# Weight pair sums moved from GpSimd to VectorE, and the step tables of a fused attention and feed-forward kernel set anew

## The chip, the cores and the metric

The kernel runs on one core of a Trainium2 chip. The metric is the device time of one execution in microseconds (us). A core has five engines that run side by side, each with its own queue of instructions in a fixed order: TensorE (PE; PEld is its weight load), VectorE (DVE), ScalarE (ACT), GpSimd (POOL) and SyncE (SP), which issues all transfers (DMA) here. An engine whose next instruction has to wait holds up all that stand behind it in its queue.

## The reference

```python
def _attn_ref(q, k, v):                       # (8, 12, 448, 64) each, float32
    scores = scale * np.matmul(q, k.transpose(0, 1, 3, 2)) - np.log(S)
    attn = 1.0 / (1.0 + np.exp(-scores))
    return np.matmul(attn, v)

def _moe_ref(x, w_ch1, w_ch2):                # x (8, 448, 768), w 768x3072 and 3072x768
    X = np.fft.fft(np.fft.fft(x, axis=1), axis=2)
    u = x + np.real(X)
    un = (u - mean(u)) / np.sqrt(var(u) + 1e-06)
    return u + np.maximum(un @ w_ch1, 0.0) @ w_ch2
```

The weights arrive as float64 and are read as pairs of 32-bit words. Sigmoid attention over 96 heads, a real part of a two-dimensional Fourier transform, a row norm and a two-layer feed-forward net follow each other.

## The kernel before

**First part, to about 365 us.** A loop over even ticks `t` (one tick is one 128-row block of scores) issues per round: last round's stores (`sp_next`), last round's ACT reads (`act_next`), a list of small steps that the table `extra` holds for this tick (sorted by rank), the scores, the values, and some matmuls of the Fourier stage. Into the same ticks go the loads of the weights' words (`weight_load`, tile `wr`, L400), a running maximum of each (`weight_max`, L408), and for 30 weight blocks the conversion from float64 to float32 in three steps (`convert`: ACT L416, DVE L418, DVE L421) into a tile `t` of three buffers, from where it is stored to `t_dram` (L433). A new conversion can start on ACT only when the store of the third last one has landed. `STORES` says for the stores of `u` and of `t` whether they join `sp_next` (issued at the start of the next round) or `sp_later` (one round after that). The norm of the first 512 rows (`NORMS`, `token_norm` with c = 0) ends in four pairs of DMA transposes (L591), issued from SP as well. The Fourier stage's results go from PSUM through ACT (`A`, L331; `Q`, L342) and DVE (`u`, L368).

**Second part, 365 to 400 us.** The rest of the Fourier stage runs beside the first up projections; a list `prepq` feeds one weight step per round.

**Third part, from 400 us.** The work is cut into blocks `P`, each of 14 ticks: seven ticks issue an up projection (`fast_up`, nine matmuls of 256 columns, `psf`, L1073), the others a down projection (`down_plain`, `po`, L946, for the first 512 rows; `fast_down`, `pso`, L1145, after that). `UPS`, `PIECES` and `DOWN_TICKS` say which tick issues what. Products go through two PSUM banks (`a` and `b`): ACT copies (`X`, L1088; `F`, L1095) and DVE sums (`F`, L1084) must read a bank before TensorE may write to it again, a few ticks later; so a late ACT or DVE stops TensorE.

The up and down products use sums and differences of weight quarters. These pair sums (`pair_sum`, L634, four for each pair of weight blocks, 128x384 float32, both inputs in SBUF) run on GpSimd: 10 pairs by `w1_pair` (tile `t`), 2 by `w1_rest` (tile `tp`), 12 by `w2_sums` (tile `cb`); 96 in all. After them comes a scaled float16 copy on ACT (`high`, L623) and its remainder on DVE (`low`, L626, tile `ws`). `to_float32` turns the words of further blocks on the way (`w1_turn`, L416, L418, L421 with tile `r`). GpSimd also does the small norm operations (`mv`, L516 to L540) of the later rows.

Where each of these steps stands is set by tables of tick numbers: `at_tick(P, k, fn)` puts a step at tick `k` of block `P` (negative: before it), and within a tick by the fraction. Blocks 2 to 11 handle the first 512 rows (to about 545 us), blocks 12 to 23 the next 512 rows with the second weight's pair sums made on the way, and from block 24 on (about 724 us) all weights are loaded ready-made.

Of the kernel before, what the change touches and what calls it, by code (L numbers as in the profile page):

```python
# [13 lines left out]
ALU = mybir.AluOpType  # L14
# [44 lines left out]
TICKS = 14  # L59
DOWN_TICKS = (1, 3, 5, 7, 9, 10, 13)  # L60
DOWN_FROM = 5
STORES = (1, 1)
MAX_STEP = (0, 0, 0, 0, 0, -4.0, 0, 0, 0, 0, 0, 0, 0, 0, 0, 0, 0, 0, 0, 0, 0, 0, 0, 4.0, 0, 0, 0, 0, 0, 0, 0, 0, 0, 0, 0, 0, 0, 0, 0, 0, 0, 0, 0, 0, 0, 0, 4.0, 0)
CONV_STEP = (0, 2, 4, 0, 2, 4, 0, 2, 4, 0, 2, 4, 0, 2, 4, 0, 0.0, 4, 0, 2, 4, 0, 2, 4, 0, 2, 4, 0, 2, 4, 0, 2, 4, 0, 2, 4, 0, 2, 4, 0, 2, 4, 0, 2, 4, 0, 2, 2.0, 0, 2, 4, 0, 2, 4, 0, 2, 4, 0, 2, 4, 0, 2, 4, 0, 2, 4, 0, 2, 4, 0, 2, 4, 0, 2, 4, 0, 2, 4, 0, 2, 4, 0, 2, 4, 0, 2, 4, 0, 2, 4, 0, 2, 4, 0, 2, 4, 0, 2, 4, 0, 2, 4, 0, 2, 4, 0, 2, 4, 0, 2, 4, 0, 2, 4, 0, 2, 4, 0, 2, 4, 0, 2, 4, 0, 2, 4, 0, 2, 4, 0, 2, 4, 0, 2, 4, 0, 2, 4, 0, 2, 4, 0, 2, 4)
CONV_RANK = (4, 8.0, 14.0)
CAST_STEP = (0, 0, 0, 0, 0, 0, 0, 0, 0, 0, 0, 0, 0, 0, 0, 0, 0, 0, -2.0, 0, 0, 0, 0, 0, 0, 0, 0, 0, 0, 0, 0, 0, 0, 0, 0, 0, 0, 0, 0, 0, 0, 0, 0, 0, 0, 0, 0, 0, 0, 0, 0, 0, 0, 0, 0, 0, 0, 0, 0, 0, 0, 0, 0, 0, 0, 0, 0, 0, 0, 0, 0, 0, 0, 0, 0, 0, 0, 0, 0, 0, 0, 0, 0, 0, 0, 0, 0, 0, 0, 0, 0, 0, 0, 0, 0, 0)
W1P_AT = (1.25, 3, 4, 5.75, 6, 6.25, 9.0, 11.0, 13.0)
TURN_AT = (2, 4, 4.0, 5.75, 8.0, 8.0)
WORDS_AT = (4.0, 2.5)
W2P_AT = (-4.75, 8.0, 8.0, 9.0)  # L70
# [18 lines left out]
def spectral_attention_ffn(tc, q, k, v, w1, w2, cd, cs, ident_in, out):  # L89
    nc = tc.nc  # L90
# [7 lines left out]
    with ExitStack() as top:  # L98
# [19 lines left out]
        if True:  # L118
# [433 lines left out]
            def token_norm(c, tp, n, rows_in, stage, dma, e):  # L552
# [63 lines left out]
            prep = {}  # L616
# [229 lines left out]
        with ExitStack() as fast, ExitStack() as plain, ExitStack() as pairs, ExitStack() as words_in:  # L846
# [24 lines left out]
            def w1_pair(p, n):  # L871
                t = prep[0, p]
# [18 lines left out]
            def w1_rest(p, n):  # L891
# [26 lines left out]
            def w2_sums(P, n):  # L918
# [448 lines left out]
```

## Time and profile before

| | |
|---|---|
| median of 3 runs | 1572.38 us (1570.44 to 1575.49) |
| profiled execution, whole | 1571.36 us |
| its span, first to last instruction | 1569.6 us |
| busy share: PE, PEld, DVE, ACT, POOL | 98%, 68%, 71%, 51%, 23% |
| mean granted TensorE clock | 0.996 |

The span is 1.76 us shorter than the execution it belongs to; what lies around it is taken as the same for both kernels. The profile is read by stretches of time, since the five parts have different limits: a busy share over the whole span mixes them.

### The profile page before, as it was taken

How to read it: one execution, taken by the hardware profiler on the slowest of the kernel's cores; microseconds unless marked ns; L12 is line 12 of the kernel's file. 1: busy time of each engine (PE TensorE's matmuls, PEld its weight loads, DVE VectorE, ACT ScalarE, POOL GpSimd, SP SyncE). 2: the span in 40 equal slices, each digit the busy share in tenths (PEclk: the TensorE clock that was granted, in tenths of full speed). 3: DMA queues.
4: the chain of work that ended last, by engine and by line, in shares of the span. 5: the costliest groups of instructions: out<-in, count | busy, mean ns of one | idle time of the engine just before them, and what ended most of it. 6: DMA issues, size and time to landing. Idle time of an engine off the chain costs nothing.

```text
span 1569.6 us, 27940 instructions
## 1 busy us (share of the span) xinstructions
PE 1534.7 (98%) x11338; PEld 1067.9 (68%) x11338; DVE 1119.4 (71%) x1802; ACT 795.4 (51%) x1125; POOL 367.8 (23%) x446
## 2 busy tenths in 40 slices
PE   9999999899999999999999999999999999999998
PEld 4555555455667676777777777777777777777775
DVE  2668878777788856887767676767666766766567
ACT  6777777673566536543544244533543364324231
POOL 3645656541344625240000000000000000000000
PEclk9999999999999999999999999999999999999999
DMA  7878798955898998997797578667857676856544
GB/s 236 318 272 301 232 363 288 311 205 183 319 288 323 288 353 295 324 259 272 260 275 213 208 305 236 232 222 286 257 224 235 259 258 238 270 228 235 198 173 151
DMA packets 162996, 407.83 MB, mean 260 GB/s; under 512 B 87489, under 2 KB 101554, under 8 KB 144690
## 3 DMA queue, kind: packets, MB, share of 16 engines
q1 hardware_dynamic: 162866, 406.04, 75.8%
q8 instruction: 89, 1.46, 0.4%
q14 instruction: 41, 0.34, 0.1%
HBM read 319.49 MB, written 66.85 MB: 246 GB/s over the span
## 4 chain that ended last, share of the span: by engine, by line
PE 78%; DVE 8%; ACT 4%; POOL 4%; issue 3%; DMA 2%; SPq 1%; DVEq 0%; ACTq 0%; POOLq 0%
PE psf L1073 29%; PE pso L1145 28%; PE av L265 7%; PE sc L206 5%; PE psd L328 2%; POOL cb L634 2%; PE po L946 2%; DVE ws L626 1%; PE sc L240 1%; DVE F L1084 1%; ACT ws L623 1%; PE pss L338 1%; PE psx L361 1%; POOL t L634 1%; PE psh L656 1%
## 5 line engine op out<-in xcount | busy, mean ns | idle before, releaser
L1073 PE MATMUL psf<-ut,ws 128*128 128x256 f16 x5166 | 643.1, 273 | 14.1 <-DVE F L1084 8.4
L1073 PEld LDWEIGHTS <-ws 128*128 128x128 f16 x5166 | 505.6, 98 | 131.4 <-issue 18.6
L1145 PE MATMUL pso<-ws,H 128*128 128x384 f16 x3024 | 559.8, 326 | 1.0 <-DVE H L1084 0.9
L1145 PEld LDWEIGHTS <-H 128*128 128x128 f16 x3024 | 295.9, 98 | 154.1 <-DVE H L1084 1.7
L1159 DVE TENSOR_TENSOR acc<-pso,acc 128x384 f32<-128x384 f32 x399 | 220.4, 554 | 99.6 <-PE pso L1145 94.2
L1088 ACT ACTIVATE X<-psf 128x256 f32<-128x256 f32 x246 | 93.7, 381 | 261.0 <-PE psf L1073 260.1
L1084 DVE TENSOR_TENSOR F<-X,psf 128x256 f32<-128x256 f32 x246 | 102.6, 417 | 145.0 <-PE psf L1073 93.7
L218 ACT ACTIVATE a<-sc 128x900 f32<-128x900 f32 x168 | 148.8, 925 | 57.3 <-PE sc L206 56.9
L1084 DVE TENSOR_TENSOR H<-F,H 128x1024 f16<-128x1024 f32 (+1 forms) x144 | 156.3, 1120 | 17.3 <-ACT H L1113 17.2
L1113 ACT ACTIVATE H<-F 128x1792 f16<-128x1792 f32 x72 | 122.1, 1697 | 69.7 <-DVE F L1084 68.9
L265 PE MATMUL av<-a,vr 128*64 128x450 f32 (+1 forms) x768 | 139.9, 547 | 0.0
L529 POOL TENSOR_SCALAR mv<-mv 128x2 f32<-128x2 f32 x12 | 4.2, 346 | 564.5 <-ACT U L528 564.3
L1084 DVE TENSOR_TENSOR F<-F 128x256 f32<-128x256 f32 x288 | 109.8, 419 | 12.8 <-ACT F L1102 10.4
L199 DVE TENSOR_TENSOR lo<-qk,hi 128x834 fp32r<-128x834 f32 (+2 forms) x50 | 58.9, 1181 | 63.7 <-ACT hi L181 54.6
L265 PEld LDWEIGHTS av<-a,vr 128*64 128x64 f32 (+1 forms) x768 | 44.8, 136 | 82.0 <-issue 77.0
L1102 ACT ACTIVATE F<-F 128x768 f32<-128x768 f32 x72 | 60.7, 843 | 75.1 <-DVE F L1084 75.1
L1095 ACT ACTIVATE F<-psf 128x256 f32<-128x256 f32 x82 | 31.3, 382 | 133.0 <-PE psf L1073 133.0
L946 PE MATMUL po<-w2q,H 128*128 128x512 f16 (+1 forms) x528 | 93.5, 326 | 0.0
L289 POOL TENSOR_TENSOR eo<-xT 128x450 f32<-128x450 f32 x37 | 54.7, 1494 | 98.4 <-ACT xT L277 98.4
L634 POOL TENSOR_TENSOR t<-t 128x384 f32<-128x384 f32 x40 | 53.0, 1324 | 95.3 <-DVE ws L626 65.2
L634 POOL TENSOR_TENSOR cb<-cb 128x384 f32<-128x384 f32 x48 | 56.2, 1196 | 73.9 <-DMA cb<-t_dram 53.3
L946 PEld LDWEIGHTS <-H 128*128 128x128 f16 x528 | 51.7, 98 | 24.5
(122 smaller groups left out, 1627.5 us busy)
## 6 DMA issues: line engine op xcount, KB each, us to landing
ws<-w_dram SPq DMA_DIRECT2D x132, 1344.0 KB, 7.1
wr<-w_in SPq DMA_DIRECT2D x48, 768.0 KB, 7.2
r<-w_in SPq DMA_DIRECT2D x18, 768.0 KB, 9.6
w_dram<-ws SPq DMA_DIRECT2D x10, 1344.0 KB, 9.4
t_dram<-t SPq DMA_DIRECT2D x30, 384.0 KB, 6.6
qk<-q_in SPq DMA_DIRECT2D x48, 225.0 KB, 6.7
qk<-k_in SPq DMA_DIRECT2D x48, 224.0 KB, 5.3
vr<-v_in SPq DMA_DIRECT2D x24, 448.0 KB, 4.2
```

The costliest lines, as they stand in the source:

```text
L206: nc.tensor.matmul(ps[:, j, :SQ], split[g, kn][1][h, c * 128:(c + 1) * 128], split[g, qn][0][h], start=(n == 0), stop=(n == 2))
L218: nc.scalar.activation(a, ps[:, :, :SQ], AF.Sigmoid, bias=-math.log(S), scale=1.0 / math.sqrt(D))
L265: nc.tensor.matmul(av[1][j * D:(j + 1) * D, :SQ], vr[k, v0:v0 + D], a[k, j], start=(av[0] == 0), stop=(av[0] == 3))
L634: e.tensor_tensor(out=t[:, o], in0=t[:, x], in1=t[:, y], op=op)
L946: nc.tensor.matmul(po[n][:, at:at + hi - lo], h[:, x, j, i * 128:(i + 1) * 128], w[:, y, c0 + lo:c0 + hi], start=(p == j == m == at == 0), ...
L1073: nc.tensor.matmul(ps, w[:, i, a, m * 128:(m + 1) * 128], ut[j][:, b + (c == 0), m], start=(no in (1, 2, 5) and m == n == 0), stop=(m == n ...
L1084: nc.vector.tensor_tensor(out=o, in0=x, in1=y, op=op)
L1088: later(0, lambda: nc.scalar.activation(X[:, k], ps, AF.Copy))
L1102: nc.scalar.activation(F[:, 0:3], F[:, 0:3], AF.Relu)
L1113: nc.scalar.activation(h_tile(P)[:, 0], F[:, 1:8], AF.Copy)
L1145: nc.tensor.matmul(ps[:, :384], H[:, x, a, tp * 128:(tp + 1) * 128], w[:, y, b], start=(j == group[0] and n == 0), stop=(j == group[-1] an ...
L1159: later(0, lambda: nc.vector.tensor_tensor(out=to, in0=ps[:, :384], in1=to, op=ALU.add))
```

## The change

`ON_POOL` names, for the eight kinds of pair sum (four of the first weight, four of the second) and four kinds of norm subtraction, the engine. Only the last sum of the second weight's four stays on GpSimd; the other kinds run on VectorE. So 84 of 96 sums move, and 12 stay. (The norm subtractions were on VectorE before and stay there.) `STORES` goes from `(1, 1)` to `(0, 0)`. All tables of ticks for weight, norm and conversion steps get new numbers; `PIECES` moves two down pieces of the first-row blocks from tick 5 to tick 3.

```diff
-NORMS = ((66, 74, 76, 80, 84, 88, 94), (108, 114, 116, 120, 124, 128, 134))
+NORMS = ((66, 74, 76, 80, 86, 88, 94), (108, 114, 116, 116, 124, 124, 136))
...
-STORES = (1, 1)
+STORES = (0, 0)
+ON_POOL = (0, 0, 0, 0, 0, 0, 0, 1, 0, 0, 0, 0)
...
-CONV_RANK = (4, 8.0, 14.0)
+CONV_RANK = (4, 10.0, 16.0)
...
-TURN_AT = (2, 4, 4.0, 5.75, 8.0, 8.0)
+TURN_AT = (2, 3.75, 4.0, 6.75, 9.0, 10.0)
 WORDS_AT = (4.0, 2.5)
-W2P_AT = (-4.75, 8.0, 8.0, 9.0)
-REST_AT = (-12.25, 0, 0.0, 3.0, 3, 5, 7, 9)
+W2P_AT = (-5.75, 6.25, 8.0, 9.75)
+REST_AT = (-12.25, 0, 0.0, 0.0, 3, 5, 6.0, 8.0)
 RESID_AT = (3, 8)
-SUMS_AT = (-4, 2, 3.0, 6, 8, 10, 10, 11.25, 15.25)
-SUMS2_AT = (-17.0, -10.0, -7.75, -5.0, -3.0, 2.0, 6.25, 9.75, 12.75)
-LOAD_AT = (8.25, 2.0, -2.0)
+SUMS_AT = (-5.0, 2, 3.0, 6, 8, 10, 10, 11.25, 14.25)
+SUMS2_AT = (-19.0, -9.25, -7.0, -4.25, -2.25, 2.0, 7.0, 10.5, 13.5)
+LOAD_AT = (8.25, -4.75, -4.0)
 NORM0_AT = (6.0, 62.0)
 NORM_AT = (34.0, 90)
-NORM_STEP = (0, 13.0, 17.0, 19.0, 22.0, 22.25, 23.5, 29.25, 29.5, 31.25, 33.25, 34.5, 36.5, 41.5, 43.5)
-PIECES = {1: 0, 3: 0, 5: 5, 7: 1, 10: 5, 13: 1}
+NORM_STEP = (0, 13.0, 17.0, 22.0, 25.0, 25.25, 28.5, 32.25, 32.5, 34.25, 36.25, 37.5, 39.5, 44.5, 49.5)
+PIECES = {1: 0, 3: 2, 5: 3, 7: 1, 10: 5, 13: 1}
...
+            def eng(n):
+                return (nc.vector, nc.gpsimd)[ON_POOL[n]]
...
-                    pair_sum(0, t, n - 2, nc.gpsimd)
+                    pair_sum(0, t, n - 2, eng(n - 2))
...
-                    pair_sum(0, prep[0, p], n - 1, nc.gpsimd)
+                    pair_sum(0, prep[0, p], n - 1, eng(n - 1))
...
-                    pair_sum(1, prep[1, P], n - 1, nc.gpsimd)
+                    pair_sum(1, prep[1, P], n - 1, eng(n + 3))
```

The left-out lines are tables with a number for each of 48 weight maxima, 144 conversion steps and 96 casts, of which six, two and none change in value. In the changed file, lines after 62 stand one further down, lines after the new function `eng` four.

The first place is SP's queue near the second pair of transposes of the second norm block (some 287 to 298 us in the trace). `t_3044` is a converted weight block; before the change its store stood here:

```order
L400 DMA wr<-w_in 128x1536
L591 DMA_TRANSPOSE ut<-un_3083 128x12x128 x2
L172 DMA vr<-v_in 128x896
L400 DMA wr<-w_in 128x1536
L433 DMA t_dram<-t_3044 128x768
L166 DMA qk<-k_in 128x448
L167 DMA qk<-q_in 128x450
L433 DMA t_dram<-t_3085 128x768
```

In the changed kernel the same block is called `t_3048` and the transposes take `un_3131`:

```order
L401 DMA wr<-w_in 128x1536
L434 DMA t_dram<-t_3048 128x768
L173 DMA vr<-v_in 128x896
L401 DMA wr<-w_in 128x1536
L595 DMA_TRANSPOSE ut<-un_3131 128x12x128 x2
L434 DMA t_dram<-t_3086 128x768
L167 DMA qk<-k_in 128x448
L168 DMA qk<-q_in 128x450
```

The store of this block has moved from behind the two transposes to ahead of them, and ahead of two loads; the next store (`t_3085`, now `t_3086`) stands behind the transposes in both.

The second place is DVE's queue in the blocks of the first 512 rows, from the first half of `low` to the second bank-freeing sum `F<-X,psf` after it (`t_` and a number is a weight pair on its way, `r` the words it is made from, `w2q` the second weight's copy, `U` the norm's rows). Before, in block 4 (some 433 to 447 us):

```order
L626 SCALAR_TENSOR_TENSOR ws<-t_4394,wsc,ws 128x1152
L418 TENSOR_SCALAR t_4570<-t_4570 128x768
L421 SCALAR_TENSOR_TENSOR t_4570<-r,t_4570 128x768
L418 TENSOR_SCALAR t_4570<-t_4570 128x768
L421 SCALAR_TENSOR_TENSOR t_4570<-r,t_4570 128x768
L626 SCALAR_TENSOR_TENSOR w2q<-t_4477,wsc,w2q 128x1536
L574 TENSOR_TENSOR U<-U 128x384 x2
L1084 TENSOR_TENSOR F<-X,psf 128x256
L626 SCALAR_TENSOR_TENSOR ws<-t_4394,wsc,ws 128x1536
L574 TENSOR_TENSOR U<-U 128x384 x2
L1084 TENSOR_TENSOR F<-X,psf 128x256
```

In the changed kernel:

```order
L630 SCALAR_TENSOR_TENSOR ws<-t_4394,wsc,ws 128x1152
L419 TENSOR_SCALAR t_4557<-t_4557 128x768
L638 TENSOR_TENSOR t_4394<-t_4394 128x384
L422 SCALAR_TENSOR_TENSOR t_4557<-r,t_4557 128x768
L638 TENSOR_TENSOR t_4394<-t_4394 128x384 x3
L630 SCALAR_TENSOR_TENSOR w2q<-t_4469,wsc,w2q 128x1536
L419 TENSOR_SCALAR t_4557<-t_4557 128x768
L1088 TENSOR_TENSOR F<-X,psf 128x256
L422 SCALAR_TENSOR_TENSOR t_4557<-r,t_4557 128x768
L630 SCALAR_TENSOR_TENSOR ws<-t_4394,wsc,ws 128x1536
L578 TENSOR_TENSOR U<-U 128x384 x2
L1088 TENSOR_TENSOR F<-X,psf 128x256
```

Four sums (L638) now stand ahead of the first of these two bank-freeing sums, the two halves of the words' turn (L419, L422) are drawn apart, and the norm's first two subtractions have moved behind that bank-freeing sum.

The third place is DVE's queue in block 14, the first even block in which the second weight's sums (`cb`) are made while the earlier ones run out (some 583 to 597 us). Before:

```order
L1084 TENSOR_TENSOR F<-X,psf 128x256
L1084 TENSOR_TENSOR F<-F 128x256 x4
L1084 TENSOR_TENSOR F<-X,psf 128x256
L1084 TENSOR_TENSOR H<-F,H 128x1024
L1084 TENSOR_TENSOR H<-F,H 128x768
L1084 TENSOR_TENSOR F<-X,psf 128x256
L626 SCALAR_TENSOR_TENSOR ws<-cb,wsc,ws 128x1536
L1084 TENSOR_TENSOR F<-X,psf 128x256
```

In the changed kernel:

```order
L1088 TENSOR_TENSOR F<-X,psf 128x256
L1088 TENSOR_TENSOR F<-F 128x256 x4
L638 TENSOR_TENSOR cb<-cb 128x384
L1088 TENSOR_TENSOR F<-X,psf 128x256
L638 TENSOR_TENSOR cb<-cb 128x384
L1088 TENSOR_TENSOR H<-F,H 128x1024
L638 TENSOR_TENSOR cb<-cb 128x384
L1088 TENSOR_TENSOR H<-F,H 128x768
L638 TENSOR_TENSOR cb<-cb 128x384 x2
L1088 TENSOR_TENSOR F<-X,psf 128x256
L638 TENSOR_TENSOR cb<-cb 128x384
L630 SCALAR_TENSOR_TENSOR ws<-cb,wsc,ws 128x1536
```

Six sums of two weight pairs now stand among the bank-freeing sums; the two that close each set of four are still on GpSimd.

## Rows read from the trace of the kernel before

**Rows 1.** Busy time per engine by stretch: us, busy us, granted clock, DMA share, GB/s.

```profile
0.00:365.00 365.00, 351.57 (x2411) 192.26 (x2412) 260.81 (x340) 263.60 (x340) 197.27 (x170) 0.99 0.81 274
365.00:400.00 35.00, 32.29 (x196) 20.94 (x195) 25.81 (x39) 13.92 (x17) 4.00 (x4) 1.00 0.67 226
400.00:540.00 140.00, 132.37 (x988) 96.33 (x986) 118.21 (x113) 88.88 (x112) 71.38 (x72) 1.00 0.93 309
540.00:700.00 160.00, 153.74 (x1161) 113.80 (x1159) 113.10 (x173) 81.08 (x119) 57.90 (x73) 0.99 0.92 306
700.00:1520.00 820.00, 820.00 (x6286) 614.80 (x6284) 564.73 (x1072) 338.57 (x528) 37.26 (x128) 1.00 0.71 245
```

**Rows 2.** TensorE's own waits: engine, line, releaser, us in total, times, longest.

```profile
PE psf L1073 <- DVE F L1084: 8.4, 11, 1.6
PE psf L1073 <- ACT X L1088: 4.5, 7, 2.3
...
PE pss L338 <- ACT A L331: 3.7, 1, 3.7
```

**Rows 3.** Timeline 286 to 306: start, us, engine, line, tiles, idle before and releaser.

```profile
286.60 0.95 DVE L421 SCALAR_TENSOR_TENSOR t<-wr,t 128x768 int32<-128x768 int32 x1
...
287.45 7.23 SPq L591 DMA_TRANSPOSE ut<-un  x2
...
296.52 0.42 SPq L433 DMA_DIRECT2D t_dram<-t  x1
...
302.24 0.89 ACT L416 ACTIVATE t<-wr 128x768 f32<-128x768 f32 x1 [5.79 <-DMA t_dram<-t]
```

**Rows 4.** Busy time per engine, two short stretches with a lower clock.

```profile
304.00:308.00 4.00, 3.62 (x14) 2.27 (x14) 1.73 (x3) 4.00 (x7) 3.92 (x3) 0.50 1.04 410
...
600.00:604.00 4.00, 4.00 (x23) 2.57 (x22) 2.51 (x4) 3.67 (x6) 0.00 (x0) 0.65 1.02 404
```

**Rows 5.** Pair sums on GpSimd and a like VectorE row: busy us, mean ns.

```profile
L634 POOL TENSOR_TENSOR cb<-cb 128x384 f32<-128x384 f32 x48 | 56.2, 1196 | 73.9 <-DMA cb<-t_dram 53.3 <-DVE acc L1159 19.6
...
L634 POOL TENSOR_TENSOR t<-t 128x384 f32<-128x384 f32 x40 | 53.0, 1324 | 95.3 <-DVE ws L626 65.2 <-DMA u_dram<-u 27.9
...
L1199 DVE TENSOR_TENSOR acc<-acc 128x384 f32<-128x384 f32 x70 | 38.5, 550 | 0.2
```

**Rows 6.** Conversion's last step, whole run: shortest, median, longest ns.

```profile
L421 DVE SCALAR_TENSOR_TENSOR t<-r,t x18: 959/1633/1643, 395.9 to 520.6; 128x768 int32<-128x768 int32 x18
```

**Rows 7.** VectorE groups, 400 to 700: busy us, mean ns, idle before.

```profile
L421 DVE SCALAR_TENSOR_TENSOR t<-r,t 128x768 int32<-128x768 int32 x16 | 23.5, 1467 | 0.5
...
L1084 DVE TENSOR_TENSOR H<-F,H 128x768 f16<-128x768 f32 x9 | 11.7, 1305 | 0.0
```

**Rows 8.** The same table, 700 to 1520, with GpSimd nearly idle.

```profile
L1084 DVE TENSOR_TENSOR H<-F,H 128x768 f16<-128x768 f32 x60 | 57.8, 964 | 0.0
```

**Rows 9.** Timeline 437.5 to 446.5, columns as in rows 3.

```profile
438.08 1.95 ACT L543 ACTIVATE U<-U,mv 128x768 f32<-128x768 f32 x2 [2.62 <-POOL mv L540]
...
441.53 2.33 DVE L626 SCALAR_TENSOR_TENSOR w2q<-t,wsc,w2q 128x1536 f16<-128x1536 f32 x1 [3.54 <-ACT w2q L623]
...
445.30 1.14 PE L1073 MATMUL psf<-ut,ws 128*128 128x256 f16 x9 [1.59 <-DVE F L1084]
```

**Rows 10.** Timeline 585 to 600, columns as in rows 3.

```profile
586.08 9.72 POOL L634 TENSOR_TENSOR cb<-cb 128x384 f32<-128x384 f32 x8 [17.89 <-DMA cb<-t_dram]
...
593.80 1.57 ACT L623 ACTIVATE ws<-cb,wsc 128x1536 f16<-128x1536 f32 x1 [4.79 <-POOL cb L634]
...
595.41 2.00 DVE L626 SCALAR_TENSOR_TENSOR ws<-cb,wsc,ws 128x1536 f16<-128x1536 f32 x1 [5.03 <-ACT ws L623]
...
599.32 0.97 PE L1073 MATMUL psf<-ut,ws 128*128 128x256 f16 x4 [2.27 <-ACT X L1088]
```

**Rows 11.** Waits of SyncE's DMA queue, columns as in rows 2.

```profile
SPq L400 <- DVE t L421: 28.9, 8, 7.9
```

**Rows 12.** The page's DMA issues: KB each, median us to landing.

```profile
ws<-w_dram SPq DMA_DIRECT2D x132, 1344.0 KB, 7.1
```

More of the change, by code (lines that the diff above doesn't have):

```diff
@@ L61 @@
 DOWN_FROM = 5
-STORES = (1, 1)
-MAX_STEP = (0, 0, 0, 0, 0, -4.0, 0, 0, 0, 0, 0, 0, 0, 0, 0, 0, 0, 0, 0, 0, 0, 0, 0, 4.0, 0, 0, 0, 0, 0, 0, 0, 0, 0, 0, 0, 0, 0, 0, 0, 0, 0, 0, 0, 0, 0, 0, 4.0, 0)
-CONV_STEP = (0, 2, 4, 0, 2, 4, 0, 2, 4, 0, 2, 4, 0, 2, 4, 0, 0.0, 4, 0, 2, 4, 0, 2, 4, 0, 2, 4, 0, 2, 4, 0, 2, 4, 0, 2, 4, 0, 2, 4, 0, 2, 4, 0, 2, 4, 0, 2, 2.0, 0, 2, 4, 0, 2, 4, 0, 2, 4, 0, 2, 4, 0, 2, 4, 0, 2, 4, 0, 2, 4, 0, 2, 4, 0, 2, 4, 0, 2, 4, 0, 2, 4, 0, 2, 4, 0, 2, 4, 0, 2, 4, 0, 2, 4, 0, 2, 4, 0, 2, 4, 0, 2, 4, 0, 2, 4, 0, 2, 4, 0, 2, 4, 0, 2, 4, 0, 2, 4, 0, 2, 4, 0, 2, 4, 0, 2, 4, 0, 2, 4, 0, 2, 4, 0, 2, 4, 0, 2, 4, 0, 2, 4, 0, 2, 4)
@@ L65 @@
-CONV_RANK = (4, 8.0, 14.0)
-CAST_STEP = (0, 0, 0, 0, 0, 0, 0, 0, 0, 0, 0, 0, 0, 0, 0, 0, 0, 0, -2.0, 0, 0, 0, 0, 0, 0, 0, 0, 0, 0, 0, 0, 0, 0, 0, 0, 0, 0, 0, 0, 0, 0, 0, 0, 0, 0, 0, 0, 0, 0, 0, 0, 0, 0, 0, 0, 0, 0, 0, 0, 0, 0, 0, 0, 0, 0, 0, 0, 0, 0, 0, 0, 0, 0, 0, 0, 0, 0, 0, 0, 0, 0, 0, 0, 0, 0, 0, 0, 0, 0, 0, 0, 0, 0, 0, 0, 0)
+STORES = (0, 0)
+ON_POOL = (0, 0, 0, 0, 0, 0, 0, 1, 0, 0, 0, 0)
+MAX_STEP = (0, 0, 0, 0, 0, -4.0, 0, 0, -2.0, 0, 0, 0, 0, 0, 0, 0, 0, -4.0, 0, 0, 0, 0, 0, 4.0, 2.0, 0, 0, 0, 0, 0, 0, 0, 0, 0, 0, 0, 0, 0, 0, 0, 0, 0, 0, 4.0, -2.0, 0, 4.0, 4.0)
@@ new lines @@
+CONV_STEP = (0, 2, 4, 0, 2, 4, 0, 2, 4, 0, 2, 4, 0, 2, 4, 0, 0.0, 4, 0, 2, 4, 0, 2, 4, 0, 2, 4, 0, 2, 4, 0, 2, 4, 0, 2, 4, 0, 2, 4, 0, 2, 4, 0, 2, 4, 0, 2, 2.0, 0, 2, 4, 0, 2, 4, 0, 2, 4, 0, 2, 4, 0, 2, 4, 0, 2, 4, 0, 2, 4, 0, 2, 4, 0, 2, 4, 0, 2, 4, 0, 2, 4, 0, 2, 4, 0, 2, 4, 0, 2, 4, 0, 2, 4, 0, 2, 4, 0, 2, 4, 0, 2, 4, 0, 2, 4, 0, 2, 4, 0, 2, 2.0, 0, 2, 4, 0, 2, 4, 0, 2, 4, 0, 2, 4, 0, 4.0, 4, 0, 2, 4, 0, 2, 4, 0, 2, 4, 0, 2, 4, 0, 2, 4, 0, 2, 4)
+CONV_RANK = (4, 10.0, 16.0)
+CAST_STEP = (0, 0, 0, 0, 0, 0, 0, 0, 0, 0, 0, 0, 0, 0, 0, 0, 0, 0, -2.0, 0, 0, 0, 0, 0, 0, 0, 0, 0, 0, 0, 0, 0, 0, 0, 0, 0, 0, 0, 0, 0, 0, 0, 0, 0, 0, 0, 0, 0, 0, 0, 0.0, 0, 0, 0, 0, 0, 0, 0, 0, 0, 0, 0, 0, 0, 0, 0, 0, 0, 0, 0, 0, 0, 0, 0, 0, 0, 0, 0, 0, 0, 0, 0, 0, 0, 0, 0, 0, 0, 0, 0, 0, 0, 0, 0, 0, 0)
@@ L572, in token_norm @@
                 elif n < 11:
-                    for o, x, y in (((4, 0, 2), (5, 1, 4)), ((6, 1, 0), (7, 3, 5)))[n - 9]:
-                        nc.vector.tensor_tensor(out=U[:, o], in0=U[:, x], in1=U[:, y], op=ALU.subtract)
+                    for k, (o, x, y) in enumerate((((4, 0, 2), (5, 1, 4)), ((6, 1, 0), (7, 3, 5)))[n - 9]):
+                        (eng(2 * n + k - 10) if c else nc.vector).tensor_tensor(out=U[:, o], in0=U[:, x], in1=U[:, y], op=ALU.subtract)
                 else:
```

## The prediction

> **What bounds the kernel now.** I read first the busy time by stretch [rows 1]. TensorE is the engine that sets the end: from 700 us on it is busy for 820.0 of 820.0 us, so nothing can be won there. Its idle time lies in the earlier stretches: 13.4 us to 365, 2.7 to 400, 7.6 to 540 and 6.3 to 700, together 30 us, beside some at the end that the change does not touch. So the change can win about 2% of the span at most, and it wins only what it takes from these four stretches.
>
> Then I asked what ended TensorE's waits [rows 2]. After 400 us it waits for a PSUM bank that DVE or ACT has not yet read: 8.4 us for DVE's sums `F`, 4.5 us for ACT's copies `X`. In the first part one wait of 3.7 us stands out, for ACT's copy `A`.
>
> Its cause is in the timeline [rows 3]. ACT wanted to start a conversion and found no free buffer: it sat idle for 5.79 us until a store of `t` had landed, and the copy `A` stood behind it in its queue. DVE had finished that block at 287.55 (286.60 plus 0.95), but SP issued its store only at 296.52, since two transposes kept SP's queue for 7.23 us from 287.45 on. After the pause the granted clock was 0.50, so TensorE ran at 1.2 instead of 2.4 GHz for 304 to 308, which loses 2.0 us more; after the pause near 597 us it was 0.65 for 4 us, a loss of 1.4 us [rows 4].
>
> After 400 us DVE is the tight engine: busy 118.2 of 140 us, then 113.1 of 160 [rows 1]. In block 4 the chain is: ACT waits 2.62 us for GpSimd's norm operations, so `w2q` on DVE starts 3.54 us late, the sum `F` stands behind it, and TensorE stops for 1.59 us [rows 9]. In block 14 it is GpSimd's sums: eight of `cb` take 9.72 us from the landing of their load, ACT waits 4.79 us for them, DVE 5.03 us for ACT, and TensorE stops for 2.27 us behind a copy that stood after this [rows 10].
>
> **The change part by part.**
>
> *The sums.* 84 of 96 sums leave GpSimd, where one takes 1.32 us (`t`) or 1.20 us (`cb`) [rows 5]. On DVE the nearest row is an addition of the same shape with both inputs in SBUF, 0.55 us [rows 5]. Four belong to the pair done before 400 us, so 80 come to DVE between 400 and 710 us: 44 us. Two weight chains become shorter by this: four sums took some 4 x 1.2 to 1.3 us, and take 2.2 us of DVE time.
>
> *What DVE gets back.* While GpSimd works, DVE's operations with two SBUF inputs take longer: the conversion's last step takes 959 ns at best and 1633 ns in the median [rows 6]; its mean between 400 and 700 us is 1467 ns for 16, so 8.1 us are lost there [rows 7]. The 768-element remainder of `H` takes 1305 ns there and 964 ns where GpSimd is nearly idle: 9 x 0.34 = 3.1 us [rows 7, 8]. These two groups give 11 us, the lower bound; if each of the 80 sums cost its neighbours what the conversion step shows on average (0.51 us), it is 41 us. I take 20, nearer to the lower end, since many of DVE's operations there read PSUM and GpSimd often ran beside those. DVE's load then rises by 24 us (3 to 33), from 231 to 255 of 300 us.
>
> The Trainium skill, "SBUF — State Buffer", section "Who interferes with whom", says that a DVE instruction with two SBUF inputs and a GpSimd instruction that reads SBUF exclude each other for a whole instruction. By that rule a sum could hold DVE up for all of its time and more would come back than I take; the trace agrees in the sign, and its 0.67 us between best and median [rows 6] is less than a sum's length.
>
> *Blocks 2 to 11, 400 to 540 us (7.6 us idle).* About 42 of the moved sums fall here: 118.2 + 42 x 0.55 - about 14 of the 20 us = 127 of 140 us. That fits, but with little room. What TensorE loses there are not averages but long or late operations ahead of `F`. Without sums on GpSimd its norm operations have nothing of that kind beside or ahead of them, the scaling stands three ticks later, and the norm's subtractions no longer stand ahead of the bank-freeing sum in block 4: the 1.59 us wait [rows 9] and its like go. `PIECES` gives ACT's copy of the first product two pieces' time before its bank is written again. I take 5 of 7.6 us; the bounds are 7.6 won and 8 lost (DVE full, below).
>
> *Blocks 12 to 22, 540 to 700 us (6.3 us idle, 1.4 us of clock).* The sums of each `cb` pair cost DVE 1.65 us and GpSimd about 1 us, in place of 9.72 us for two pairs in a row, so ACT no longer waits 4.79 us [rows 10]. What is late next is the load itself: a sum on DVE waits for `cb` with the bank-freeing sums behind it, where before only GpSimd waited (17.89 us, harmless by itself) [rows 10]. That load landed at 586.08, about when the block's first sum is due, and its issue now stands one or two ticks earlier; I expect waits under 1 us. An even block holds six sums (3.3 us) and an odd one none, and the norm's steps move to the odd ones. DVE: 113.1 + 21 - 6 = 128 of 160 us. I take 4.5 of 7.7 us; bounds 7.7 won, 3 lost.
>
> *The stores.* With `STORES` at 0 a store is issued one round earlier. The block of [rows 3] is stored ahead of the two transposes, so some 6 to 9 us earlier, and the wait of 5.79 us goes. But the next block's store stays behind the transposes, and without the pause its buffer is wanted sooner; I expect a shorter wait of ACT there. Of 3.7 us [rows 2] and 2.0 us of clock I take 4.2; bounds 0 and 5.7. The rest of the idle 13.4 us is DVE being late by about a microsecond at a time; the new places of maxima and norm steps shift that, I take nothing, and 4 us either way as bounds.
>
> *365 to 400 us.* Four sums (2.2 us) come onto DVE, which was busy 25.8 of 35 us [rows 1]; the earlier stores of `u` free its buffers sooner. Together nothing, with 2 us either way.
>
> *The steady stretch.* `LOAD_AT` puts two weight loads next to each other. A load of 1344 KB lands in 7.1 us [rows 12], and two blocks of TensorE work lie between issue and use; DMA is busy for 0.71 there [rows 1]. Hidden; if a load were late it would show as a wait of TensorE for `ws`, and each us counts fully. The later norm steps there lie beside a DVE that is 69% busy.
>
> *Sum:* 4.2 + 5 + 4.5 + 0 = 13.7 us. From the profiled execution's 1571.36 us that leaves 1557.7; the runs' median is 1.0 us above that execution, so 1558.7, and I say 1558.5 us.
>
> **The rivals.**
>
> *DVE becomes the bound (slower).* Place: blocks 2 to 11. If nothing comes back of DVE's lengthened operations, its work is 118.2 + 23.1 = 141 us in a stretch of 140, and part of its idle 21.8 us, in which it waits for ACT in order, cannot be filled. With half of it kept, the stretch takes 152 us: 12 lost instead of 5 won. The rest unchanged but for the stores (4.2) and nothing won in blocks 12 to 22, the time is 1572.4 + 12 - 4.2 = 1580. It decides from the point where DVE's added work there exceeds what it has idle beyond those waits, about 11 us net. For it: 84% busy already. Against it: the lengthened steps of [rows 6, 7].
>
> *The move changes nothing.* What GpSimd waited for, DVE now waits for, and stops go to other places. Blocks 2 to 22 keep their 14 us, only the stores win: 1568. The Trainium skill, "Perfetto Trace Analysis", section "Optimizing Scalar/DVE Operations", warns that moving work between these two engines might not help, as they share a read port. That rule would end here; the rows of the lengthened operations [rows 7, 8] rather speak for the one that pays less being DVE alone.
>
> *The stores give back what they win.* They now stand ahead of loads and hold SP until DVE has finished a block; such waits were 28.9 us in 8 already, the longest 7.9 [rows 11]. If the loads of `qk` behind them come late, the 4.2 us won become some 4 lost: 1567. Against it: those loads were issued long ahead, and none is named among TensorE's waits.
>
> *All of it is won.* If every sum gives DVE back 0.51 us or more, its load falls or stays, and all 7.6, 7.7 and 5.7 us go, perhaps 3 more of the first part: 1572.4 - 24 = 1548.
>
> **How the numbers follow.** My forecast (1552 to 1566) has 0.42. All won: 0.16, faster. The stores give back: 0.12, at the edge of faster. Nothing changes: 0.14, counted as the same. DVE full: 0.16, slower. A measurement of this kernel can tell 0.3% (4.7 us) from no change, so faster is below 1567.7 and slower above 1577.1: 0.70, 0.14 and 0.16. The range from 1547 to 1576 leaves out most of the last case and a little at the lower end.
>
> **What would show it.** Right: no 5.79 us wait of ACT for a store and a granted clock near 1.00 between 300 and 312; the conversion's step near 0.96 us after 400; waits of `psf` for DVE and ACT of a few us together; still 100% of TensorE's time busy in the steady stretch, begun some 13 us earlier. Wrong: DVE busy for over 95% between 400 and 540 with more waits of `psf` behind it; sums of `cb` on DVE waiting for their load; waits for `ws` loads after 700 us; or another store that lands late.

## The result, and the profile after

| | before | after |
|---|---|---|
| median | 1571.79 us (1570.44 to 1575.49, 4 runs) | 1548.56 us (1547.14 to 1549.52, 4 runs) |
| profiled execution, its span | 1571.36, 1569.6 | 1549.52, 1547.7 |
| busy share PE, DVE, POOL | 98%, 71%, 23% | 99%, 73%, 17% |
| mean granted clock | 0.996 | 0.998 |

The ratio is 0.985 (95% interval 0.983 to 0.987): 23.2 us won, where 13.9 were forecast. The time lies 1.6 us above the lower end of the stated range, and below the 1552 to 1566 us that my own sum had for itself.

Busy time by stretch of the changed kernel, columns as in [rows 1]:

```profile
0.00:365.00 365.00, 358.35 (x2477) 199.26 (x2478) 266.61 (x350) 267.56 (x346) 196.26 (x170) 1.00 0.83 280
365.00:400.00 35.00, 33.41 (x200) 20.62 (x199) 28.49 (x42) 14.14 (x17) 0.00 (x0) 1.00 0.79 273
400.00:540.00 140.00, 137.58 (x1033) 101.32 (x1031) 119.97 (x154) 91.86 (x115) 14.13 (x30) 0.99 0.95 319
540.00:700.00 160.00, 157.67 (x1214) 118.45 (x1212) 132.01 (x227) 84.84 (x121) 23.42 (x42) 1.00 0.93 310
700.00:1520.00 820.00, 819.76 (x6288) 614.81 (x6286) 560.02 (x1072) 338.03 (x527) 33.18 (x120) 1.00 0.71 243
```

TensorE's idle time in the four stretches was 13.4, 2.7, 7.6 and 6.3 us; it is 6.7, 1.6, 2.4 and 2.3. The steady stretch is full as before. DVE's load from 400 to 700 us rose from 231 to 252 us. That stretch holds more of the work than before, since all of it starts earlier. Over the whole execution DVE is busy for 1130.6 us instead of 1119.4: the 84 sums bring 46 us, and 11 us remain, so some 35 us were given back.

Fixed bounds shift against the work, so I also cut the run at events of TensorE. The view of one line's instructions gives each line's first and last start (us, behind the shortest, median and longest time in ns); first in the kernel before, then in the changed one:

```profile
L265 PE MATMUL av<-a,vr x768: 535/541/959, 10.8 to 360.7; 128*64 128x450 f32 x144, 64*64 64x450 f32 x48
L1073 PE MATMUL psf<-ut,ws x5166: 269/273/417, 399.1 to 1538.8; 128*128 128x256 f16 x199
L946 PE MATMUL po<-w2q,H x528: 272/326/379, 408.6 to 580.1; 128*128 128x512 f16 x88, 128*128 128x256 f16 x88
L1145 PE MATMUL pso<-ws,H x3024: 322/326/524, 588.4 to 1565.6; 128*128 128x384 f16 x189
```

```profile
L266 PE MATMUL av<-a,vr x768: 535/541/769, 11.1 to 352.4; 128*64 128x450 f32 x144, 64*64 64x450 f32 x48
L1077 PE MATMUL psf<-ut,ws x5166: 269/273/422, 389.0 to 1517.0; 128*128 128x256 f16 x199
L950 PE MATMUL po<-w2q,H x528: 272/326/631, 398.4 to 563.9; 128*128 128x512 f16 x88, 128*128 128x256 f16 x88
L1149 PE MATMUL pso<-ws,H x3024: 322/326/337, 572.7 to 1543.9; 128*128 128x384 f16 x189
```

In the changed kernel the last value product starts at 352.4 us, the first up product at 389.0, the last down product of the first rows at 563.9, and the last one of all at 1543.9. So the four parts were 360.7, 38.4, 181.0 and 985.5 us long and are now 352.4, 36.6, 174.9 and 980.0: won are **8.3 us** in the first part, **1.8** in the second, **6.1** in blocks 2 to 11, **5.5** after them. The third cut lies at the last down product of the first rows, some 24 to 40 us behind the 540 us of the forecast, so the third part takes in some of the stretch of blocks 12 to 22. These parts are used for every run below; each comes from the one execution that was profiled.

TensorE's waits, columns as in [rows 2]:

```profile
PE psf L1077 <- ACT X L1092: 3.1, 3, 2.2
PE psx L362 <- DVE u L369: 2.9, 3, 2.0
PE psf L1077 <- DVE F L1088: 1.9, 3, 1.2
PE psi L709 <- DVE u L706: 1.7, 1, 1.7
...
PE sc L207 <- DVE lo L200: 0.8, 1, 0.8
```

The wait of `pss` for the copy `A` is gone, and the waits for `F` went from 8.4 to 1.9 us. The timeline answers to [rows 3]:

```profile
284.12 0.38 SPq L434 DMA_DIRECT2D t_dram<-t  x1
...
287.07 9.96 SPq L595 DMA_TRANSPOSE ut<-un  x2
...
294.18 0.91 ACT L417 ACTIVATE t<-wr 128x768 f32<-128x768 f32 x1
...
297.13 0.53 SPq L434 DMA_DIRECT2D t_dram<-t  x1
```

The store now leaves before the two transposes, although these hold SP for 9.96 us. The next one leaves at 297.13 behind them, as I had feared, but the next waits of ACT for a landed store are short, 0.48 and 1.08 us. The granted clock was 1.00 from 292 to 312, against 0.50 at 304 to 308 [rows 4].

DVE's rows, once by shortest, median and longest ns over the whole run ([rows 6], and the sums), once as groups from 400 to 700 us ([rows 7]):

```profile
L422 DVE SCALAR_TENSOR_TENSOR t<-r,t x18: 943/951/962, 386.9 to 507.9; 128x768 int32<-128x768 int32 x18
L638 DVE TENSOR_TENSOR t<-t x40: 541/556/559, 375.5 to 521.2; 128x384 f32<-128x384 f32 x40
L638 DVE TENSOR_TENSOR cb<-cb x36: 544/550/1019, 542.9 to 684.6; 128x384 f32<-128x384 f32 x36
```

```profile
L1088 DVE TENSOR_TENSOR F<-X,psf 128x256 f32<-128x256 f32 x64 | 26.6, 415 | 19.7 <-ACT X L1092 10.4 <-PE psf L1077 9.3
L638 DVE TENSOR_TENSOR cb<-cb 128x384 f32<-128x384 f32 x36 | 19.7, 563 | 1.2 <-DMA cb<-t_dram 0.8 <-issue 0.3
L630 DVE SCALAR_TENSOR_TENSOR w2q<-t,wsc,w2q 128x1536 f16<-128x1536 f32 x10 | 18.1, 1813 | 5.7 <-ACT w2q L627 5.7
L422 DVE SCALAR_TENSOR_TENSOR t<-r,t 128x768 int32<-128x768 int32 x15 | 14.3, 951 | 0.0
L1088 DVE TENSOR_TENSOR H<-F,H 128x768 f16<-128x768 f32 x11 | 10.4, 949 | 0.0
```

The conversion's step went from a median of 1633 ns to 951, with no long one left. A sum costs 0.55 us, as taken, and the sums of `cb` waited 0.8 us in all for their loads.

### The profile page after: what moved, and what is told of

Its sections match the earlier page's. It is cut to its first block, busy times and chain, and to the rows that moved or that the text cites. A ratio compares the mean times of both kernels' runs of the same rounds, so it can differ in the third digit from the quotient of the medians.

```text
span 1547.7 us, 27944 instructions
## 1 busy us (share of the span) xinstructions
PE 1529.9 (99%) x11338; PEld 1067.6 (69%) x11338; DVE 1130.6 (73%) x1886; ACT 798.1 (52%) x1125; POOL 267.0 (17%) x362
## 4 chain that ended last, share of the span: by engine, by line
PE 92%; DVE 3%; DMA 2%; ACT 1%; issue 1%; SPq 0%; DVEq 0%; ACTq 0%
PE psf L1077 35%; PE pso L1149 31%; PE av L266 8%; PE sc L207 6%; PE po L950 5%; PE psd L329 3%; PE sc L241 2%; PE pss L339 1%; PE psx L362 1%; DMA u_dram<-u 1%; DMA U<-u_dram 1%; DVE F L1088 1%; DVE u L369 0%; DMA r<-w_in 0%; DMA qk<-q_in 0%
## 5 line engine op out<-in xcount | busy, mean ns | idle before, releaser
L1088 DVE TENSOR_TENSOR H<-F,H 128x1024 f16<-128x1024 f32 (+1 forms) x144 | 151.5, 1084 | 11.2 <-ACT H L1117 10.9
L207 PE MATMUL sc<-hi 64*128 64x450 f32 x288 | 62.0, 428 | 0.5 <-ACT a L219 0.4
L1161 ACT ACTIVATE acc<-pso 128x384 f32<-128x384 f32 x84 | 40.0, 482 | 34.9 <-PE pso L1149 34.9
```

Source lines behind the costliest of these rows:

```text
L207: nc.tensor.matmul(ps[:, j, :SQ], split[g, kn][1][h, c * 128:(c + 1) * 128], split[g, qn][0][h], start=(n == 0), stop=(n == 2))
L1088: nc.vector.tensor_tensor(out=o, in0=x, in1=y, op=op)
```

## The experiments

Three questions: does GpSimd's work lengthen DVE's, or was it the longer chain of waits; what do stores, steps and later tables win each; and which later table matters? Medians are given with the ratio to the kernel before, run beside each group (1573.4 us in each of the three groups; 1571.8 beside the changed kernel, so differences between groups are uncertain by about 1.6 us). Each kernel is the changed file with some of its tables set back; with all tables of before it has the order of before.

**1. Only the sums move.**

```diff
 # the kernel before, with
+ON_POOL = (0, 0, 0, 0, 0, 0, 0, 1, 0, 0, 0, 0)
```

> The kernel before with one thing changed: 84 of 96 pair sums on VectorE, at the old places; all tables as before. Theory A (the engine of the sums is what wins in blocks 2 to 22): the idle time of TensorE after its first up product of the blocks falls by most of the 11.7 us that it fell by in the changed kernel, time 1559 to 1563, and the conversion's last step takes 0.96 us between 400 and 540 us. Rival B (the new places win, and sums on VectorE at the old ones make it late for its bank-freeing sums): 1568 to 1580, with more waits of psf for DVE.

Measured: 1567.62 us, ratio 0.996 (0.995 to 0.998): 5.8 won, less than A and just better than B. Its profiled execution is the longest of its eight (1570.14 us). Its parts are 364.7, 38.3, 176.2 and 984.9: the sums won 4.8 us in blocks 2 to 11 and 0.6 after them. Four microseconds more in the first part, where the order is that of before, are mostly two waits of TensorE behind ACT's `xT` (3.3 us) in that one execution. From 400 to 700 us `F` was still waited for:

```profile
PE psf L1077 <- DVE F L1088: 7.8, 11, 1.7
PE psf L1077 <- ACT X L1092: 1.9, 3, 1.5
```

**2. All but the sums' engine.**

```diff
 # the changed kernel, with
-ON_POOL = (0, 0, 0, 0, 0, 0, 0, 1, 0, 0, 0, 0)
+ON_POOL = (1, 1, 1, 1, 1, 1, 1, 1, 0, 0, 0, 0)
```

> The changed kernel with all 96 pair sums back on GpSimd, at the new places. Theory A: the 11.7 us of blocks 2 to 22 are lost again, 1558 to 1562, and the conversion's last step takes 1.4 us on average or more. Rival B: the places are worth most of it, 1549 to 1553.

Measured: 1563.76 us, ratio 0.994 (0.992 to 0.995). Theory A, and somewhat beyond it: at the new places the engine is worth some 14 us (9.7 won here against 23.2). Blocks 2 to 11 take 184.0 us, 3.0 more than before the change: the new places suit sums on DVE, and hurt with sums on GpSimd. The conversion's step is long again, the sum that reads PSUM (`F<-X,psf`) is not:

```profile
L1088 DVE TENSOR_TENSOR F<-X,psf 128x256 f32<-128x256 f32 x61 | 25.2, 413 | 17.8 <-ACT X L1092 12.6 <-PE psf L1077 5.1
L422 DVE SCALAR_TENSOR_TENSOR t<-r,t 128x768 int32<-128x768 int32 x15 | 20.1, 1339 | 0.2
```

Not only operations with two inputs in SBUF are longer. The conversion's middle step (`TENSOR_SCALAR`, which reads `t` alone) is, too; from 390 to 700 us, by shortest, median and longest ns, here and in the changed kernel:

```profile
L419 DVE TENSOR_SCALAR t<-t x16: 551/1346/1359, 393.9 to 511.9; 128x768 int32<-128x768 int32 x16
L419 DVE TENSOR_SCALAR t<-t x16: 546/552/555, 394.7 to 507.1; 128x768 int32<-128x768 int32 x16
```

**3. Only the stores.**

```diff
 # the kernel before, with
-STORES = (1, 1)
+STORES = (0, 0)
```

> The kernel before with STORES at (0, 0) alone. My theory: the wait of ACT for a landed store near 300 us and the lower clock behind it go or shrink, 4 to 6 us won, 1566 to 1568. Rival (the first part won its 8.3 us by the new places of norm and maximum steps, and the stores alone only move the wait to the next block): 1571 to 1573.

Measured: 1566.87 us, ratio 0.996 (0.994 to 0.997), 6.5 won, as expected. Parts: 357.9, 36.6, 181.8, 986.0, of the slowest of its six executions (1568.04 us), so they show only 3.3 us of the 6.5. The first part won 2.8 us: the 3.7 us wait went, but a wait of 0.7 us behind ACT's `xT` came, and after two waits of 1.0 us each the granted clock fell elsewhere, here to half:

```profile
280.00:284.00 4.00, 4.00 (x21) 3.20 (x24) 3.94 (x6) 1.10 (x1) 0.00 (x0) 0.50 1.18 309
```

The cause is not the one I had forecast. The store of the block of [rows 3] is still behind the two transposes:

```profile
286.91 7.97 SPq L595 DMA_TRANSPOSE ut<-un  x2
294.99 0.53 SPq L434 DMA_DIRECT2D t_dram<-t  x1
```

It is now the first in SP's queue behind them, ahead of two loads: 7.5 us after DVE has finished the block (at 287.51 us), where it was 9.0 us before. The conversion that waited 5.79 us for it now starts after 1.24 us, put down to DVE, and the one after it waits 2.08 us for its store. In this execution a store that was 1.5 us less late was enough.

The second part won 1.8 us, for which I had taken nothing: the waits of `psx` for `u` between 365 and 400 us went from 2.1 us in three to 0.6 in one, with the earlier stores of `u`.

**4 and 5. The first part's tables, with and without the stores.** Both are the kernel before with the changed `NORMS`, `MAX_STEP`, `CONV_STEP` and `CONV_RANK`.

```diff
 # 4: also
-STORES = (1, 1)
+STORES = (0, 0)
```

Of 4:

> The kernel before with the tables of the first part (stores, norm of the first rows, maxima, conversions) from the changed kernel; sums and all later tables as before. If the parts are independent: 8.3 us won to the last value product and 1 to 2 us behind it, 1561 to 1564. Rival (the later part gives some back, since its start shifts against the loads): 1565 to 1570.

Of 5:

> The kernel before with the changed tables of the first part except the stores: norm, maximum, conversion and cast steps moved, the stores of u and t as late as before, sums and all later tables as before. Additive theory (the places win what the first-part run won beyond the stores run): about 6.9 us, from the waits near 188, 259, 275 and 278 us, so 1564 to 1567 us, with the 3.7 us wait of TensorE for ACT's copy A still there. Rival (the places win only because the stores no longer hold ACT up; with the late stores the stop for the copy A grows or moves and takes it back): 1569 to 1574 us.

Measured: 4 gives 1559.94 us, ratio 0.992 (0.990 to 0.993), better than expected; 5 gives 1566.19 us, ratio 0.996 (0.994 to 0.997), as the additive theory has it. The steps alone won 7.2 us, the stores alone 6.5, both 13.5: they add up. Waits to 400 us, first three of the kernel before, then three of 5:

```profile
PE sc L206 <- DVE lo L199: 2.1, 2, 1.1
...
PE psd L328 <- DVE u L368: 1.0, 1, 1.0
PE psd L328 <- DVE xp L308: 1.0, 1, 1.0
```

```profile
PE psx L362 <- DVE u L369: 3.8, 5, 1.9
PE psi L709 <- DVE u L706: 1.7, 1, 1.7
...
PE sc L207 <- DVE lo L200: 0.8, 1, 0.8
```

The waits of `psd` are gone and that for `lo` is shorter; three short waits (0.5 to 0.9 us) for ACT and a load have come. The 3.7 us wait for `A` [rows 2] is gone too, with `STORES` as before, which I had not expected. The timeline of 5 says why:

```profile
284.84 0.45 SPq L434 DMA_DIRECT2D t_dram<-t  x1
...
286.68 8.87 SPq L595 DMA_TRANSPOSE ut<-un  x2
```

With the moved steps DVE finishes the block at 283.39 us, and its store leaves ahead of the two transposes, as in the changed kernel. So it is the steps that put the store ahead of the transposes, and not `STORES`; either alone ends the wait for `A`, each in its own way. What the late stores keep is the waits for `u` in the second part (37.9 us in 5, 36.6 in 4).

**6. Idle sums on GpSimd.**

```diff
 # the changed kernel; gd is a tile of 128x384 float32 of its own (its two lines are left out)
                 e.tensor_tensor(out=t[:, o], in0=t[:, x], in1=t[:, y], op=op)
+                if e is nc.vector:
+                    nc.gpsimd.tensor_tensor(out=gd[0], in0=gd[0], in1=gd[0], op=ALU.subtract)
```

> The changed kernel, and for each sum on VectorE GpSimd also makes an addition of the same size (128x384 float32) of a tile of its own, whose result nobody reads and nobody waits for. All sums that the kernel needs stay on VectorE at the changed places. My theory (GpSimd's sums cost above all by lengthening VectorE's operations with two inputs in SBUF): the conversion's last step goes from about 0.96 back towards 1.5 us, waits of psf for VectorE and ACT come back between 400 and 700 us, and the time rises by half or more of what the sums on GpSimd cost at these places (about 14 us): 1555 to 1562 us. Rival (what cost was that ACT and VectorE waited for sums that take 1.2 us instead of 0.55, a longer chain): nobody waits for these, so the time stays within 2 us of the changed kernel's, 1547 to 1551 us.

Measured: 1579.6 us, ratio 1.0045 (1.003 to 1.006): the theory's sign, and more than twice its size; the rival falls. 84 additions that nobody needs cost 31 us and make the kernel slower than before the change. DVE is busy for 1164.3 us instead of 1130.6, with the same operations. In the profile 23 of 30 us are longer waits of TensorE; the rest is its own longer busy time, with a granted clock of 0.94 from 400 to 540 us against 0.99. The loss begins ahead of block 2: 7.7 us of it are in the second part, beside the first nine additions (rows in 7). DVE's own sums now collide:

```profile
L640 DVE TENSOR_TENSOR t<-t x40: 546/557/1183, 380.6 to 545.4; 128x384 f32<-128x384 f32 x40
...
L422 DVE SCALAR_TENSOR_TENSOR t<-r,t x18: 945/953/1578, 391.9 to 530.6; 128x768 int32<-128x768 int32 x18
```

Waiting for nothing, the additions run in rows, so most of DVE's operations meet none and the medians hardly move; I had expected the conversion's median to. Where a row falls, it falls on one operation behind the other, `F<-X,psf` excepted (414 ns on average). Timeline around the longest wait between 400 and 700 us:

```profile
514.03 13.58 POOL L642 TENSOR_TENSOR gd<-gd 128x384 f32<-128x384 f32 x10
...
520.96 1.18 DVE L640 TENSOR_TENSOR t<-t 128x384 f32<-128x384 f32 x1
...
523.55 3.37 DVE L640 TENSOR_TENSOR t<-t 128x384 f32<-128x384 f32 x3
...
526.96 1.58 ACT L627 ACTIVATE ws<-t,wsc 128x1536 f16<-128x1536 f32 x1 [5.11 <-DVE t L640]
...
530.71 1.65 PE L1083 MATMUL psf<-ut,ws 128*128 128x256 f16 x7 [5.04 <-DVE F L1094]
```

Ten additions on GpSimd, sums on DVE at 1.18 and 1.12 us instead of 0.55, a bank-freeing sum behind them, and TensorE stops for 5.04 us.

**7. Idle fills in their place.** The same GpSimd time, without reading.

```diff
                 if e is nc.vector:
-                    nc.gpsimd.tensor_tensor(out=gd[0], in0=gd[0], in1=gd[0], op=ALU.subtract)
+                    for _ in range(3):
+                        nc.gpsimd.memset(gd[0], 1.0)
```

> The changed kernel, and for each sum on VectorE GpSimd fills a tile of its own (128x384 float32) three times, about the time of one addition, reading nothing and with nobody waiting for it. It is the idle-sums run with work that only writes. Theory 1 (idle sums cost because two engines read two inputs each from SBUF): the fills leave VectorE's operations at their length (conversion's last step about 0.96 us, sums about 0.56), and what they cost is only the norm steps behind them in GpSimd's queue: 1549 to 1560 us, at most half of what the idle sums cost (31 us). Theory 2 (idle sums cost because GpSimd's queue is full and the norm's small operations come late): about as much as the idle sums, 1570 to 1582 us.

Measured: 1554.72 us, ratio 0.988 (0.987 to 0.990): theory 1. 252 fills (107.8 us of GpSimd, where the 84 additions took 99.3) cost 6 us, a fifth of what the additions cost. DVE is busy for 1131.8 us, 1.2 more than in the changed kernel, and its sums and last conversion steps are no longer:

```profile
L640 DVE TENSOR_TENSOR t<-t x40: 537/556/564, 373.2 to 522.6; 128x384 f32<-128x384 f32 x40
...
L422 DVE SCALAR_TENSOR_TENSOR t<-r,t x18: 945/952/969, 384.5 to 509.7; 128x768 int32<-128x768 int32 x18
```

One of the one-input steps took 0.87 us instead of 0.55, and the rest stayed at 0.55 to 0.59. The clearest pair of rows is that of the same two DVE operations near 353 us, beside the first nine additions of 6 and beside the first 27 fills:

```profile
353.36 2.41 DVE L290 TENSOR_TENSOR eo<-xT 128x450 f32<-128x450 f32 x2
352.31 1.16 DVE L290 TENSOR_TENSOR eo<-xT 128x450 f32<-128x450 f32 x2
```

Beside the additions they and the operations after them take up to about twice as long, and TensorE waits 5.0 us for DVE's `xp`; beside the fills it does not wait there.

DVE waits 6.1 us for `U`, scaled by ACT from GpSimd's norm values, a wait the changed kernel does not have: the norm's steps come late behind the fills. That fits the 6 us but was not tried apart; in 6 some of the 31 us may be lost in this way too.

**8 to 11. One later table back at a time**, each on the changed kernel.

```diff
 # 8: the norm steps of the later rows (NORM_STEP) as before
 # 9: the second weight's sums and the loads (SUMS_AT, SUMS2_AT, LOAD_AT) as before
 # 10: the turns, first copies and last pairs (TURN_AT, W2P_AT, REST_AT) as before
 # 11:
-PIECES = {1: 0, 3: 2, 5: 3, 7: 1, 10: 5, 13: 1}
+PIECES = {1: 0, 3: 0, 5: 5, 7: 1, 10: 5, 13: 1}
```

Of 8:

> The changed kernel with the norm steps of the later rows at the ticks of before. My prediction's step (the norm's subtractions stand ahead of the bank-freeing sum in block 4 and its like, and the later places free TensorE of that wait): stops for the sum F come back, of 1 to 1.6 us near blocks 4 and 8 and in even blocks after 12, 1551 to 1556 us. Rival (with the sums off GpSimd the norm's operations come early enough at either place): 1547 to 1550 us.

Of 9:

> The changed kernel with the second weight's sums and the loads of ready weights at the ticks of before. Theory (sums on VectorE need their load one or two ticks earlier, or VectorE stands still for it with bank-freeing sums behind): VectorE waits for the load of cb come back and TensorE stops between 540 and 700 us, 1551 to 1556 us. Rival (the load is in time at either place): 1547 to 1550 us. In the steady stretch nothing changes by either.

Of 10:

> The changed kernel with the words' turns, the second weight's first copies and the last pairs of the first weight at the ticks of before. Theory (in blocks 2 to 11 VectorE has little room once it makes the sums, and long operations must be drawn apart so that no bank-freeing sum stands behind a row of them): stops for F and X come back between 400 and 560 us, 1551 to 1557 us. Rival (room enough at either place): 1547 to 1550 us.

Of 11:

> The changed kernel with the table of the down pieces in the first-row blocks as before (two pieces back from tick 3 to tick 5). My prediction's step (the pieces at tick 3 give ACT's copy of the first product time before its bank is written again): waits of psf for the copy X come back in blocks 2 to 11, some 0.3 us in most of ten blocks, 1550 to 1555 us. Rival (with the sums off GpSimd the copies are in time anyway): within 1.5 us of the changed kernel, 1547 to 1550 us.

Measured: 8 gives 1551.54 us (ratio 0.986), 9 gives 1549.34 (0.985), 10 gives 1547.27 (0.984), 11 gives 1547.76 (0.984), beside 1548.56 of the changed kernel. Only the norm's places can be told from nothing: 3.0 us by the medians, 1.4 by what each won against the kernel before beside it. Its profile shows the loss after block 11 (982.1 against 980.0 us), not in blocks 2 to 11 (174.6 against 174.9): TensorE waits for `F` at 632 and at 668 us, 0.99 and 0.31 us, where the changed kernel does not. For 9, 10 and 11 the rivals hold. In 9 the waits of DVE for loads of `cb` do come back, as the theory had it (4.3 us in four, against 0.8), but the time does not follow.

**12. All 96 sums on DVE.**

```diff
 # the changed kernel, with
-ON_POOL = (0, 0, 0, 0, 0, 0, 0, 1, 0, 0, 0, 0)
+ON_POOL = (0, 0, 0, 0, 0, 0, 0, 0, 0, 0, 0, 0)
```

> The changed kernel with the last kind of sum, the 12 that stayed on GpSimd, on VectorE too, so that all 96 are there. Theory by the rows of the changed kernel (no stop of TensorE from 600 us to 1500 and three under 1.5 us between 540 and 600, VectorE with room there): nothing to win, 0.55 us more of VectorE per pair is covered, 1546 to 1550 us. Rival 1 (VectorE is at its limit in the even blocks): the added sums delay bank-freeing sums, 1551 to 1556 us. Rival 2 (the last sums on GpSimd are what holds up ACT's scaled copy and causes the stops near 569 to 588 us): 1544 to 1546 us.

Measured: 1548.54 us, ratio 0.984 (0.983 to 0.986): the same as the changed kernel. The last sum of each pair may stand on either engine.

## Why the prediction was right, and where its sizes were not

**What bounds it: right.** The whole win lies in the four stretches named, and the steady one gave nothing (819.76 of 820 us). By the parts 21.7 us were won where the sum had 13.7; of the 8 us between them, 6 lie ahead of the first up product and 2 behind it. That the time fell into the range at all, near its end, is owed to a wide range more than to the sum.

**The stores: the right wait, the wrong cause.** "The block of [rows 3] is stored ahead of the two transposes" is true of the changed kernel, but I put it down to `STORES`. With `STORES` alone the store stays behind them (294.99 against 286.91 us, experiment 3); with the steps alone it leaves ahead (284.84 against 286.68, experiment 5). That the stores won 6.5 us for 4.2 taken does not show that step right: 1.8 of it lie in the second part, and the wait for `A` ended with a store that was 1.5 us less late.

**The first part: mis-sized.** I took 4.2 us for the stores and nothing for the places of maxima and norm steps, with 4 us either way. In the profile the first part won 8.3 us and the second 1.8. Experiments 3 to 5 split it: stores alone 6.5 us of the median, of which 1.8 in the second part, steps alone 7.2, and they add up. So the term that was too small is "the new places of maxima and norm steps shift that, I take nothing, and 4 us either way". I had treated DVE's small latenesses as noise that moving steps shuffles; the moved steps took away those of `psd`, over half of that for `lo`, and the wait for `A` as well.

**365 to 400 us: mis-sized by 1.8 us.** "The earlier stores of `u` free its buffers sooner" was the right mechanism, and I priced it at zero.

**The sums on DVE: right, and under-sized.** The two later parts won 11.6 us for 9.5 forecast (6.1 and 5.5 for 5 and 4.5, though the cut between them is not the same). I took 20 us for what DVE's lengthened operations give back; over the whole execution some 35 came. That the load from 400 to 700 us rose by 21 us, near the 24 of the forecast, is chance, since more work falls into that stretch now. One term was missing: I counted operations with two inputs in SBUF alone, and the one-input conversion step is lengthened as well, from 0.55 to 1.35 us (experiment 2). Experiments 2, 6 and 7 show the mechanism: additions on GpSimd lengthen DVE's operations on SBUF, with the same work on DVE, and fills do so hardly at all (33.7 against 1.2 us of DVE's busy time). The sum that reads one input from PSUM is not touched: 412 ns in the kernel before, 413 with the sums back on GpSimd and 415 without. The Trainium skill, "SBUF — State Buffer", section "Who interferes with whom", says of a DVE instruction with two SBUF inputs that it contends with a GpSimd instruction that reads SBUF, not with one that only writes it. The runs agree, and add a price here: 31 us against 6. They show the one-input step lengthened beside it, of which that sentence says nothing.

**The chain got shorter as forecast.** ACT's waits for sums on GpSimd between 400 and 700 us were 22.9 us in three rows of before (11.4, 11.0 and 0.5); in the changed kernel 4.9 us are left, for the sum that stayed, and 2.4 us for sums on DVE have come. What this won apart from DVE's shorter operations is not separated: experiment 2 undoes both, and experiment 6 brings back the longer operations without the chain, but with its additions in rows that the kernel before does not have.

**The places of later steps: partly wrong.** "`PIECES` gives ACT's copy two pieces' time" was worth nothing (experiment 11), nor can a gain from turns drawn apart be seen (10). The norm's later places are worth 1.4 to 3 us, but after block 11 and not where I argued from block 4 [rows 9]. As a whole the later tables matter only with the sums' engine. With sums on GpSimd they cost 3.8 us (experiment 2 against 4). With sums on DVE they win some 4 to 6: an estimate, since the 5.8 us of experiment 1 and the 13.5 of experiment 4 are 19.3 of the 23.2 us, and 1567.62 less 13.5 is 1554.1, where the changed kernel took 1548.56. That combination was not run, and the single tables sum to less; how they act together stays open.

**The rivals.** DVE is busy for 120 of 140 us from 400 to 540 us, less than the 127 forecast, so the slower case was far off. "The move changes nothing" fell to experiment 2. The stores gave nothing back. "All of it is won" came closest by its time (1548), but not by its terms: its condition, that DVE's load falls or stays, was not met, of 30 us idle 13 are left, and more was won ahead of 400 us and less behind it than it says.

## What to carry to other kernels

Before moving additions between GpSimd and DVE, look in DVE's rows for one shape with two lengths, one-input operations too, and count what the long ones cost: that is what the move gives back, and here it paid for more than half of the added work. Work for an idle engine is not free because nobody waits for it; ask what it reads. When a change of several tables ends a wait, look in the run of each table for the order that was to end it, not only for the wait. And when a list of small steps is reordered beside a nearly full engine, each wait under 1.5 us is a candidate to go: price it by its row, not at zero.

## What was not expected of the hardware

GpSimd additions that nobody waits for cost 0.37 us each (31 us for 84) in a kernel whose DVE is 73% busy, and each takes 1.0 us in the median; fills that took about the same time in all cost a fifth. The lengthening is large (a sum from 550 to 1180 ns, the conversion's last step from 950 to 1640, its one-input step from 550 to 1350) and both lengths stand side by side in one run. And the time that SP's queue is held by two DMA transposes differs from run to run: 7.23 us in [rows 3], 9.96 at the same place in the changed kernel, so a store behind them has no fixed lateness.
